# Pointwise convolution with a scaled weight: the weight set-up ahead of the main loop rewritten, and the first waits moved into the loop

## The chip, the cores and the metric

The kernel runs on one core of one Trainium2 chip. Its time is the device time of an execution in microseconds (us). A core has five engines that run side by side and wait for each other through semaphores: TensorE (PE in the profile; its weight loads are PEld), VectorE (DVE), ScalarE (ACT), GpSimd (POOL) and SyncE (SP), which here only issues DMA transfers.

## The reference

With a depthwise kernel of size 1, the padding is zero wide and the double loop runs once:

```python
H = W = 384; C = 384; k = 1           # x: (1, 384, 384, 384), dw: (1, 1, 384), pw: (384, 384), all bf16
out = out + xp[:, i:i+H, j:j+W, :] * dw[i, j][None, None, None, :]
return jnp.einsum('bhwc,cd->bhwd', out, pw)
```

So each of the 147456 pixels is a row of 384 channels, and the output row is `x * (diag(dw) @ pw)`: one matrix product of 147456 x 384 by 384 x 384. 113 MB are read and 113 MB written.

## The kernel before

**Tiles.** The pixels are cut into 288 supertiles of 512 rows. A supertile lies in SBUF with 4 rows on each of the 128 partitions. TensorE needs the channels on the partitions, so VectorE transposes it (L255) in 32 x 32 blocks of 32-bit words, each word holding two neighbouring channels. A transposed tile `T` thus has, on each group `q` of 32 partitions, channel pairs: block `b` (0 to 5) has 64 channels, and `par` (0, 1) picks the even or the odd ones. Each matmul multiplies 32 channels by the weight `w_r[32q : 32q+32, b, par, :]` and four of them, one for each `q`, run at once in the four row groups of the array, each into its own PSUM bank. Six blocks times two parities times four groups make 48 matmuls for a supertile, accumulated in PSUM.

**Main loop.** L222 to L225: 144 passes of two supertiles, the first with `T0` and PSUM set `PS[0]`, the second with `T1` and `PS[1]`. In `supertile` the matmuls of blocks 0 and 3 wait for the two halves of `T` (`s_t`), the first one for ScalarE to have emptied the PSUM set (`s_a`), and the last matmuls of blocks 2 and 5 signal `s_pe`. ScalarE copies each finished supertile from PSUM to the output tile `O` as bf16 (L296), VectorE transposes the supertile after next.

**Transfers.** SP issues, in order, `pw_n` (L131), seven loads of X of 1, 1, 2, 2, 4, 10 and 10 supertiles (L112), and then loads and stores as buffers come free. ScalarE issues the small `dw_row` (L130).

**Set-up of the weights**, the part that the change touches. `w_r` must hold `dw * pw`, with the rows permuted (even and odd channels apart) and repeated on all four partition groups:

- GpSimd fills `zero` and `ones` (L229, L230) and makes the 0/1 selection matrix `sel` with an affine select (L231).
- TensorE runs dummy matmuls on `zero` (`idle_work(2)`, L181: 16 of them), then three matmuls that turn `dw_row` into columns (L196, signal `s_df`), then 16 more dummy matmuls.
- VectorE copies the columns to `dw_f` (L273) and multiplies `sel` by them into `sel_w`, one 512-column product for each 128 rows of `pw` (L277, signal `s_sw`).
- TensorE multiplies `sel_w` and `pw_n` (L212): for each block `b` two full 128-row matmuls, of which each does the scaling, the permutation and the repetition for one parity. They wait for all of `pw_n` (`s_pw`), and blocks 4 and 5 reuse PSUM banks that must first be copied out.
- The copies from PSUM into `w_r` (`w_out`, L268), one of 768 columns for each block, are done by ScalarE for blocks 0, 2, 3, 4 and 5 and by VectorE for block 1 (`w_eng`), and signal `s_wr`.
- VectorE's first transposes stand behind its copy, in VectorE's own order.
- TensorE waits for the copies of blocks 0, 2 and 3 ahead of the loop (L221). The other waits for copies are attached to the first matmul of each block in the first supertile of a pass, so they are met in every pass and matter in the first only.

Of the kernel before, what the change touches and what calls it, by code (L numbers as in the profile page):

```python
# [7 lines left out]
BF16 = mybir.dt.bfloat16  # L8
F32 = mybir.dt.float32
# [17 lines left out]
def kernel(  # L27
# [12 lines left out]
    nc = tc.nc  # L40
    P = nc.NUM_PARTITIONS
    B, H, W, C = x.shape
    assert dw.shape[0] == 1 and dw.shape[1] == 1, "only k=1 depthwise supported"
    D = pw.shape[1]
    N = B * H * W
    assert C == 384 and D == 384 and N % 1024 == 0
    NB = C // 64
# [15 lines left out]
    consts = ctx.enter_context(tc.tile_pool(name="consts", bufs=1))  # L63
# [1 line left out]
    psum = ctx.enter_context(tc.tile_pool(name="psum", bufs=1, space=bass.MemoryType.PSUM))  # L65

    pw_n = consts.tile([P, 3, D], BF16, name="pw_n")
    ones = consts.tile([P, 4, P], BF16, name="ones")
    sel = consts.tile([P, 4, P], BF16, name="sel")
    sel_w = consts.tile([P, 3, 4, P], BF16, name="sel_w")  # L70
    w_r = consts.tile([P, NB, 2, D], BF16, name="w_r")
    dw_row = consts.tile([1, C], BF16, name="dw_row")
    dw_f = consts.tile([P, 3], F32, name="dw_f")
    warm = consts.tile([P, 3], F32, name="warm")
    zero = consts.tile([P, D], BF16, name="zero")

    Xs = [bufp.tile([P, 4 * LMAX, C], BF16, name=f"X{i}") for i in range(NR)]
    Ts = [bufp.tile([P, NB, 256], BF16, name=f"T{i}") for i in range(2)]
    Os = [bufp.tile([P, 4 * LMAX * D], BF16, name=f"O{i}") for i in range(NR)]
    PS = [psum.tile([P, 4, 512], F32, name=f"ps{s}") for s in range(2)]  # L80

    s_x = [[nc.alloc_semaphore(f"s_x{i}{k}") for k in range(max(map(len, groups[i::NR])))] for i in range(NR)]
    s_t = [[nc.alloc_semaphore(f"s_t{i}{h}") for h in range(2)] for i in range(2)]
    s_pe = nc.alloc_semaphore("s_pe")
    s_a = [nc.alloc_semaphore(f"s_a{i}") for i in range(2)]
    s_d = nc.alloc_semaphore("s_d")
    s_o = [nc.alloc_semaphore(f"s_o{i}") for i in range(NR)]
    s_dw = nc.alloc_semaphore("s_dw")
    s_pw = nc.alloc_semaphore("s_pw")
    s_df = nc.alloc_semaphore("s_df")  # L90
    s_sw = nc.alloc_semaphore("s_sw")
    s_dwf = nc.alloc_semaphore("s_dwf")
    s_sel = nc.alloc_semaphore("s_sel")
    s_w = nc.alloc_semaphore("s_w")
    s_wr = [nc.alloc_semaphore(f"s_wr{e}") for e in range(2)]
    s_seed = nc.alloc_semaphore("s_seed")
    s_zero = nc.alloc_semaphore("s_zero")

    with tc.tile_critical():  # L99
# [28 lines left out]


        nc.scalar.dma_start(dw_row[:], dw.rearrange("a e c -> a (e c)")).then_inc(s_dw, 16)  # L130
        nc.sync.dma_start(pw_n[:], pw.rearrange("(k p) d -> p k d", p=P)).then_inc(s_pw, 16)  # L131

        todo = []
        for t, (g, i, off, first, L) in enumerate(chunks):
# [9 lines left out]


        w_eng = [1, 0, 1, 1, 1, 1]
        w_done, made = [], [0, 0]
        for e in w_eng:
            made[e] += 1
            w_done.append((s_wr[e], made[e]))  # L150

        def w_ps(b):
            return PS[0 if b in (2, 3) else 1][:, 2 * (b % 2) : 2 * (b % 2) + 2, :D]


        def supertile(s, rv):
            for b in range(NB):
                for par in range(2):
                    for q in range(4):
                        if par == 0 and q == 0 and b in (0, 3):  # L160
                            nc.tensor.wait_ge(s_t[s][b // 3], rv)
                        mm = nc.tensor.matmul(  # L162
                            PS[s][:, q, :D],
                            lhsT=Ts[s][32 * q : 32 * q + 32, b, par::2],
                            rhs=w_r[32 * q : 32 * q + 32, b, par, :],
                            start=(b == 0 and par == 0),
                            stop=(b == NB - 1 and par == 1),
                            tile_position=(32 * q, 0),
                        )
                        if b == 0 and par == 0 and q == 0:  # L170
                            mm._wait_ge(s_a[s], rv)
                        elif s == 0 and q == 0 and par == 0:
                            mm._wait_ge(*w_done[b])
                        if b in (2, 5) and par == 1 and q == 3:
                            mm.then_inc(s_pe)


        def idle_work(n):
            with nc.tensor.Fori(0, n, 1) as _:
                for i in range(8):  # L180
                    nc.tensor.matmul(  # L181
                        PS[0][:, i % 4, :D],
                        lhsT=zero[32 * (i % 4) : 32 * (i % 4) + 32, 0:P],
                        rhs=zero[32 * (i % 4) : 32 * (i % 4) + 32, :],
                        start=True,
                        stop=True,
                        tile_position=(32 * (i % 4), 0),
                    )

        nc.tensor.wait_ge(s_zero, 1)  # L190
        idle_work(2)

        nc.tensor.wait_ge(s_dw, 16)
        nc.tensor.wait_ge(s_seed, 2)
        for k in range(3):
            mm = nc.tensor.matmul(  # L196
                PS[1][:, k, D : D + 1],
                lhsT=dw_row[:, P * k : P * k + P],
                rhs=ones[0:1, 0, 0:1],
                start=True,  # L200
                stop=True,
            )
        mm.then_inc(s_df)
        idle_work(2)
        nc.tensor.wait_ge(s_pw, 16)
        for b in range(NB):
            if b % 2 == 0:
                nc.tensor.wait_ge(s_sw, b // 2 + 1)
            if b >= 4:
                nc.tensor.wait_ge(*w_done[b - 4])  # L210
            for r in range(2):
                mm = nc.tensor.matmul(  # L212
                    w_ps(b)[:, r, :],
                    lhsT=sel_w[:, b // 2, 2 * (b % 2) + r, :],
                    rhs=pw_n[:, b // 2, :],
                    start=True,
                    stop=True,
                )
            mm.then_inc(s_w)
        for b in (0, 2, 3):  # L220
            nc.tensor.wait_ge(*w_done[b])  # L221
        with nc.tensor.Fori(0, NS // 2, 1) as it:  # L222
            rv = nc.tensor.to_reg(it + 1)
            for s in range(2):
                supertile(s, rv)  # L225
# [3 lines left out]
        nc.gpsimd.memset(zero[:].bitcast(U32), 0).then_inc(s_zero)  # L229
        nc.gpsimd.memset(ones[:], 1.0).then_inc(s_seed)  # L230
        nc.gpsimd.affine_select(  # L231
            out=sel[:].rearrange("p (v r) (q w) -> p v r q w", v=2, q=4),
            in_=ones[:].rearrange("p (v r) (q w) -> p v r q w", v=2, q=4),
            pattern=[[-64, 2], [-1, 2], [0, 4], [-2, 32]],
            compare_op=mybir.AluOpType.is_equal,
            fill=0.0,
            base=0,
# [8 lines left out]
        def transposes(t, j):  # L246
            g, i, off, first, L = chunks[t]
            jj = first + j
            s = jj % 2
            Xw = Xs[g % NR][:].bitcast(U32)[:, 4 * off : 4 * (off + L), :].rearrange("p (k l) c -> p k l c", l=L)  # L250
            Tw = Ts[s][:].bitcast(U32).rearrange("p b (i k) -> p b k i", k=4)
            for h in range(2):
                if h == 0 and j == 0:
                    nc.vector.wait_ge(s_x[g % NR][i], 16 * sum(len(ls) > i for ls in groups[g % NR : g + 1 : NR]))
                ins = nc.vector.transpose(  # L255
                    out=Tw[:, 3 * h : 3 * h + 3],
                    in_=Xw[:, :, j, 96 * h : 96 * h + 96].rearrange("p k (b w) -> p b k w", w=32),
                )
                if jj >= 2:
                    ins._wait_ge(s_pe, 2 * (jj - 2) + h + 1)  # L260
                ins.then_inc(s_t[s][h])

        order = [(t, j) for t in range(NT) for j in range(chunks[t][4])]

        def w_out(b):
            e = w_eng[b]
            out, in_ = w_r[:, b, :, :], w_ps(b)
            i = nc.vector.tensor_copy(out, in_) if e == 0 else nc.scalar.copy(out, in_)  # L268
            i._wait_ge(s_w, b + 1)
            i.then_inc(s_wr[e])  # L270

        nc.vector.wait_ge(s_df, 1)
        nc.vector.tensor_copy(dw_f[:].rearrange("p (k o) -> p k o", o=1), PS[1][:, 0:3, D : D + 1]).then_inc(s_dwf)  # L273
        nc.vector.wait_ge(s_sel, 1)
        nc.vector.wait_ge(s_dwf, 1)
        for k in range(3):
            nc.vector.tensor_scalar_mul(sel_w[:, k], sel[:], dw_f[:, k : k + 1]).then_inc(s_sw)  # L277
        for b in range(NB):
            w_out(b)
        transposes(*order[0])  # L280
        transposes(*order[1])

        for jj, (t, j) in enumerate(order):
            g, i, off, first, L = chunks[t]
            s = jj % 2
# [4 lines left out]
            if jj + 1 == NS:  # L290
                nq = 2
                nc.vector.wait_ge(s_o[g % NR], 16 * sum(map(len, groups[g % NR : g : NR])))
                e = nc.vector.tensor_copy(Ov[:, nq:4, j, :], PS[s][:, nq:4, :D])  # L293
# [37 lines left out]
```

## Time and profile before

| | us |
|---|---|
| median of 15 runs | 576.5 |
| lowest and highest | 575.62, 578.65 |
| profiled execution | 576.96 |
| span of its profile | 575.2 |

| engine | busy us | share of the span |
|---|---|---|
| PE | 568.2 | 99% |
| PEld | 418.7 | 73% |
| DVE | 507.5 | 88% |
| ACT | 418.9 | 73% |
| POOL | 1.7 | 0% |

The share of busy time is an average. For a change that touches the first 8 us alone, the timeline of these is what matters. The issue of DMA transfers there, by SP (start us, duration us):

```profile
1.01 0.45 SPq L131 DMA_DIRECT2D pw_n<-in_pw_dram  x1
1.53 3.90 SPq L112 DMA_DIRECT2D X<-in_x_dram  x7
```

A line of a group reads: line in the kernel, engine, operation, output and input tile, shape, number | busy time in us, mean duration of one in ns | idle time of the engine before them and what ended it. A line of the timeline reads: start, time from the first start to the last end, engine, line, operation, count, and in brackets the idle time before it. Matmuls overlap in the array, so durations of four concurrent ones are not added; the distance of their starts is the rate.

### The profile page before, as it was taken

The numbers are of one execution on the slowest core, as the hardware profiler recorded it, in microseconds if no ns is written. First come the engines' busy times: TensorE is split into PE (matmuls) and PEld (weight loads), VectorE is DVE, ScalarE is ACT, GpSimd is POOL, SyncE is SP. The second block draws the span as 40 slices with busy tenths as digits, with TensorE's granted clock in tenths as the row PEclk, the third lists the DMA queues.
The fourth block names the chain that finished last, engine by engine and source line by source line (L and its number), as shares of the span: only waits on it lengthen the run. The fifth ranks groups of instructions, "written<-read, shape, count | busy, mean of one in ns | idle before, by whom it ended". The sixth has DMA issues, their size and how long they took to land.

```text
span 575.2 us, 29707 instructions
## 1 busy us (share of the span) xinstructions
PE 568.2 (99%) x13871; PEld 418.7 (73%) x13871; DVE 507.5 (88%) x582; ACT 418.9 (73%) x296; POOL 1.7 (0%) x8
## 2 busy tenths in 40 slices
PE   8999999999999999999999999999999999999996
PEld 5777777777777777777777777777777777777774
DVE  6888898889988988898889888988898999888984
ACT  5777777777777777777777777777777777777775
POOL 1000000000000000000000000000000000000000
PEclk9999999999999999999999999999999999999999
DMA  8999999999999999999999999999999999994996
GB/s 320 432 414 420 427 412 428 432 424 401 382 425 402 383 400 426 391 406 391 430 390 396 396 432 391 391 402 421 398 381 414 410 389 395 420 392 149 389 408 264
DMA packets 25912, 226.88 MB, mean 394 GB/s; under 512 B 1197, under 2 KB 5678, under 8 KB 22062
## 3 DMA queue, kind: packets, MB, share of 16 engines
q1 hardware_dynamic: 25900, 226.79, 98.0%
q14 instruction: 9, 0.07, 0.0%
q8 instruction: 1, 0.02, 0.0%
q10 hardware_dynamic: 2, 0.00, 0.0%
HBM read 113.54 MB, written 113.25 MB: 394 GB/s over the span
## 4 chain that ended last, share of the span: by engine, by line
PE 98%; DMA 0%; ACT 0%; DVE 0%; issue 0%; POOL 0%; POOLq 0%; SPq 0%
PE ps L162 97%; PE ps L212 1%; PE ps L181 0%; DMA out_dram<-O 0%; ACT O L296 0%; DVE O L293 0%; POOL zero L229 0%; POOL warm L228 0%; POOLq L326 0%; PE ps L196 0%; SPq L99 0%
## 5 line engine op out<-in xcount | busy, mean ns | idle before, releaser
L162 PE MATMUL ps<-w_r,T 32*128 32x384 bf16 x13824 | 561.8, 321 | 0.4 <-issue 0.4
L255 DVE STREAM_TRANSPOSE T<-X 128x384 uint32<-128x384 uint32 x576 | 504.5, 877 | 56.0 <-DMA X<-in_x_dram 0.4
L162 PEld LDWEIGHTS ps<-w_r,T 32*128 32x128 bf16 x13824 | 415.9, 93 | 146.3 <-issue 0.8
L296 ACT CAST O<-ps 128x1536 bf16<-128x1536 f32 x288 | 413.6, 1436 | 148.1 <-PE ps L162 148.1
L268 ACT CAST w_r<-ps 128x768 bf16<-128x768 f32 x5 | 3.7, 811 | 2.4 <-PE ps L212 2.4
L181 PE MATMUL ps<-zero 32*128 32x384 bf16 x32 | 2.8, 516 | 1.4 <-POOL zero L229 1.4
L212 PE MATMUL ps<-pw_n,sel_w 128*128 128x384 bf16 x12 | 3.7, 498 | 0.0
L293 DVE CAST O<-ps 128x768 bf16<-128x768 f32 x1 | 1.0, 958 | 3.0 <-DMA out_dram<-O 3.0
L212 PEld LDWEIGHTS ps<-pw_n,sel_w 128*128 128x128 bf16 x12 | 1.6, 144 | 2.3 <-issue 1.7
L273 DVE COPY dw_f<-ps 128x3 f32<-128x3 f32 x1 | 0.2, 160 | 3.0 <-PE ps L196 3.0
L181 PEld LDWEIGHTS ps<-zero 32*128 32x128 bf16 x32 | 1.1, 118 | 2.0 <-issue 1.7
L241 ACT ACT_TABLE_LOAD x1 | 1.3, 1283 | 1.5 <-SPq L99 1.5
L268 DVE CAST w_r<-ps 128x768 bf16<-128x768 f32 x1 | 1.0, 958 | 1.5 <-PE ps L212 1.5
L277 DVE TENSOR_SCALAR sel_w<-sel,dw_f 128x512 bf16<-128x512 bf16 x3 | 0.9, 350 | 0.1
L231 POOL TENSOR_SCALAR_AFFINE_SELECT sel<-ones 128x512 bf16<-128x512 bf16 x1 | 0.7, 735 | 0.1
L196 PEld LDWEIGHTS ps<-ones,dw_row 1*128 1x128 bf16 x3 | 0.3, 127 | 0.3 <-issue 0.2
L230 POOL MEMSET ones<- 128x512 bf16 x1 | 0.5, 529 | 0.0
L241 ACT COPY warm<-warm 128x1 f32<-128x1 f32 x2 | 0.3, 188 | 0.0
L229 POOL MEMSET zero<- 128x192 uint32 x1 | 0.3, 258 | 0.0
L196 PE MATMUL ps<-ones,dw_row 1*128 1x1 bf16 x3 | 0.3, 174 | 0.0
L228 POOL MEMSET warm<- 128x3 f32 x1 | 0.1, 101 | 0.5 <-SPq L99 0.5
L315 POOL MEMSET const-bfloat16-1.0<- 128x1 bf16 x1 | 0.1, 101 | 0.0
(3 smaller groups left out, 0.3 us busy)
## 6 DMA issues: line engine op xcount, KB each, us to landing
X<-in_x_dram SPq DMA_DIRECT2D x26, 3840.0 KB, 20.9
out_dram<-O SPq DMA_DIRECT2D x26, 3840.0 KB, 26.4
X<-in_x_dram SPq DMA_DIRECT2D x2, 1536.0 KB, 17.6
out_dram<-O SPq DMA_DIRECT2D x2, 1536.0 KB, 14.1
X<-in_x_dram SPq DMA_DIRECT2D x3, 768.0 KB, 8.5
out_dram<-O SPq DMA_DIRECT2D x3, 768.0 KB, 8.9
X<-in_x_dram SPq DMA_DIRECT2D x1, 2304.0 KB, 19.1
out_dram<-O SPq DMA_DIRECT2D x1, 2304.0 KB, 13.0
```

The source lines that it names most:

```text
L162: mm = nc.tensor.matmul(PS[s][:, q, :D], lhsT=Ts[s][32 * q : 32 * q + 32, b, par::2], rhs=w_r[32 * q : 32 * q + 32, b, par, :], start=(b = ...
L181: nc.tensor.matmul(PS[0][:, i % 4, :D], lhsT=zero[32 * (i % 4) : 32 * (i % 4) + 32, 0:P], rhs=zero[32 * (i % 4) : 32 * (i % 4) + 32, :], s ...
L196: mm = nc.tensor.matmul(PS[1][:, k, D : D + 1], lhsT=dw_row[:, P * k : P * k + P], rhs=ones[0:1, 0, 0:1], start=True, stop=True,)
L212: mm = nc.tensor.matmul(w_ps(b)[:, r, :], lhsT=sel_w[:, b // 2, 2 * (b % 2) + r, :], rhs=pw_n[:, b // 2, :], start=True, stop=True,)
L230: nc.gpsimd.memset(ones[:], 1.0).then_inc(s_seed)
L231: nc.gpsimd.affine_select(out=sel[:].rearrange("p (v r) (q w) -> p v r q w", v=2, q=4), in_=ones[:].rearrange("p (v r) (q w) -> p v r q w" ...
L241: c = nc.scalar.copy(warm[:, s + 1 : s + 2], warm[:, 0:1])
L255: ins = nc.vector.transpose(out=Tw[:, 3 * h : 3 * h + 3], in_=Xw[:, :, j, 96 * h : 96 * h + 96].rearrange("p k (b w) -> p b k w", w=32),)
L268: i = nc.vector.tensor_copy(out, in_) if e == 0 else nc.scalar.copy(out, in_)
L277: nc.vector.tensor_scalar_mul(sel_w[:, k], sel[:], dw_f[:, k : k + 1]).then_inc(s_sw)
L293: e = nc.vector.tensor_copy(Ov[:, nq:4, j, :], PS[s][:, nq:4, :D])
L296: a = nc.scalar.copy(Ov[:, 0:nq, j, :], PS[s][:, 0:nq, :D])
```

## The change

- `pw_n` comes in three transfers of 128 rows, two issued by SP and the last by ScalarE, each with its own semaphore. Within each 128 rows the even rows go to partitions 0 to 63, the odd ones to 64 to 127.
- GpSimd makes a 128 x 128 identity `eye`; VectorE sums it over the four groups to `sel`, 128 x 32 in fp32. `sel_w` is its product with `dw_f`, repeated over the four groups by a broadcast operand: 128 columns for each 128 rows of `pw`, not 512.
- The dw columns come from twelve matmuls with 32 output partitions each, in the row order of the new `pw_n`.
- The dummy loop's body has 4 matmuls, not 8; it runs three times and once, not twice and twice.
- The weight copies are four concurrent 32-row matmuls for each 128 rows of `pw`. Each writes one of four (block, parity) pairs, so a copy out of PSUM now takes two blocks of one parity.
- The waits for the copies ahead of the loop are gone; in the first supertile of a pass, the first matmul waits for the first four copies, and blocks 4 and 5 are taken even parity first, with one wait for each parity.

```diff
-    sel = consts.tile([P, 4, P], BF16, name="sel")
-    sel_w = consts.tile([P, 3, 4, P], BF16, name="sel_w")
+    eye = consts.tile([P, P], BF16, name="eye")
+    sel = consts.tile([P, 32], F32, name="sel")
+    sel_w = consts.tile([P, 3, 4, 32], BF16, name="sel_w")
...
-        nc.sync.dma_start(pw_n[:], pw.rearrange("(k p) d -> p k d", p=P)).then_inc(s_pw, 16)
+        for k, eng in enumerate((nc.sync, nc.sync, nc.scalar)):
+            rows = pw[P * k : P * k + P, :].rearrange("(u r) d -> r u d", r=2)
+            eng.dma_start(pw_n[:, k, :], rows).then_inc(s_pw[k], 16)
...
+        w_first = {(0, 0): [(0, 1), (1, 3)], (4, 0): [(1, 4)], (4, 1): [(1, 5)]}
...
+        steps = [(b, par) for b in range(4) for par in range(2)] + [(4, 0), (5, 0), (4, 1), (5, 1)]
...
+            for b, par in steps:
+                for q in range(4):
+                    if q == 0 and par == 0 and b in (0, 3):
+                        nc.tensor.wait_ge(s_t[s][b // 3], rv)
+                    if q == 0 and s == 0:
+                        for e, v in w_first.get((b, par), []):
+                            nc.tensor.wait_ge(s_wr[e], v)
...
-                        elif s == 0 and q == 0 and par == 0:
-                            mm._wait_ge(*w_done[b])
...
-                for i in range(8):
+                for i in range(4):
...
-        idle_work(2)
-
+        idle_work(3)
+
...
+            for j in range(4):
+                r0 = P * k + 64 * (j % 2) + j // 2
                 mm = nc.tensor.matmul(
-                    w_ps(b)[:, r, :],
-                    lhsT=sel_w[:, b // 2, 2 * (b % 2) + r, :],
-                    rhs=pw_n[:, b // 2, :],
+                    PS[1][32 * j : 32 * j + 32, 0, D + k : D + k + 1],
+                    lhsT=dw_row[:, r0 : r0 + 63 : 2],
+                    rhs=ones[0:1, 0:1],
                     start=True,
                     stop=True,
+                    tile_position=(0, 32 * j),
+                )
+        mm.then_inc(s_df)
+        idle_work(1)
+        for k in range(3):
+            nc.tensor.wait_ge(s_pw[k], 16)
+            nc.tensor.wait_ge(s_sw, k + 1)
+            if k == 2:
+                nc.tensor.wait_ge(*w_done[0])
+                nc.tensor.wait_ge(*w_done[1])
+            for j in range(4):
+                mm = nc.tensor.matmul(
+                    PS[(k + 1) % 2][:, j, :D],
+                    lhsT=sel_w[32 * j : 32 * j + 32, k, :, :].rearrange("p q w -> p (q w)"),
+                    rhs=pw_n[32 * j : 32 * j + 32, k, :],
+                    start=True,
+                    stop=True,
+                    tile_position=(32 * j, 0),
                 )
             mm.then_inc(s_w)
-        for b in (0, 2, 3):
-            nc.tensor.wait_ge(*w_done[b])
...
+            out, in_ = w_r[:, 2 * k : 2 * k + 2, r, :], w_ps(i)
...
+            o._wait_ge(s_w, k + 1)
...
+        nc.vector.tensor_reduce(
+            out=sel[:],
+            in_=eye[:].rearrange("p (q w) -> p w q", q=4),
+            op=mybir.AluOpType.add,
+            axis=mybir.AxisListType.X,
+        ).then_inc(s_dwf)
         nc.vector.wait_ge(s_df, 1)
-        nc.vector.tensor_copy(dw_f[:].rearrange("p (k o) -> p k o", o=1), PS[1][:, 0:3, D : D + 1]).then_inc(s_dwf)
...
+        nc.vector.tensor_copy(dw_f[:], PS[1][:, 0, D : D + 3]).then_inc(s_dwf)
+        nc.vector.wait_ge(s_dwf, 2)
         for k in range(3):
-            nc.vector.tensor_scalar_mul(sel_w[:, k], sel[:], dw_f[:, k : k + 1]).then_inc(s_sw)
+            nc.vector.tensor_scalar_mul(
+                sel_w[:, k], sel[:].unsqueeze(1).to_broadcast([P, 4, 32]), dw_f[:, k : k + 1]
+            ).then_inc(s_sw)
```

In the new file the main loop's matmul is L168 (before L162), the dummy work L185 (L181), the dw matmuls L202 (L196), the weight copies' matmuls L219 (L212); the loop stands at L228 (L222). The program that results has, per pass of the loop, three stand-alone waits on TensorE as before: two at its head and one ahead of the second supertile (before: one at the head, one at block 3, one ahead of the second supertile). The waits attached to matmuls go from eight to six.

## The prediction

> **What bounds the kernel now.** I read the chain of waits of the whole execution first, then the groups of instructions, then the first 9 us piece by piece.
>
> ```profile
> PE 98%; DMA 0%; ACT 0%; DVE 0%; issue 0%; POOL 0%; POOLq 0%; SPq 0%
> PE ps L162 97%; PE ps L212 1%; PE ps L181 0%; DMA out_dram<-O 0%; ACT O L296 0%; DVE O L293 0%; POOL zero L229 0%; POOL warm L228 0%; POOLq L326 0%; PE ps L196 0%; SPq L99 0%
> ...
> L162 PE MATMUL ps<-w_r,T 32*128 32x384 bf16 x13824 | 561.8, 321 | 0.4 <-issue 0.4
> L255 DVE STREAM_TRANSPOSE T<-X 128x384 uint32<-128x384 uint32 x576 | 504.5, 877 | 56.0 <-DMA X<-in_x_dram 0.4
> ```
>
> The main loop (L162) is 97% of the chain and TensorE idles 0.4 us before it in all: once started it never waits. 561.8 us over 144 passes is 3.90 us a pass, or 162.5 ns for each four concurrent matmuls. So the end moves only if the loop starts at another time, runs at another rate, or the tail after it changes. The start-up, from the chain cut at 9 us (start, duration, what):
>
> ```profile
> 1.43 1.46 PE ps L181 x12
> 2.89 0.03 PE ps L196
> 2.92 1.30 PE ps L181 x10
> 4.22 3.67 PE ps L212 x12
> 7.88 0.39 issue
> 8.27 0.81 PE ps L162 x13
> ```
>
> Dummy work, the little dw matmuls, dummy work, the weight copies, 0.39 us of loop entry; the loop starts at 8.27. Beside it, the timelines of ScalarE and VectorE:
>
> ```profile
> 5.01 0.80 ACT L268 CAST w_r<-ps 128x768 bf16<-128x768 f32 x1 [1.94 <-PE ps L212]
> 6.29 2.91 ACT L268 CAST w_r<-ps 128x768 bf16<-128x768 f32 x4 [0.48 <-PE ps L212]
> ...
> 5.65 0.96 DVE L268 CAST w_r<-ps 128x768 bf16<-128x768 f32 x1 [1.52 <-PE ps L212]
> 6.59 6.71 DVE L255 STREAM_TRANSPOSE T<-X 128x384 uint32<-128x384 uint32 x8
> ```
>
> The loop entry stands behind ScalarE's third copy (ended 7.79). The first half of the first transposed tile was ready at 7.46. It started at 6.59 for two reasons at once: VectorE's copy ended at 6.61, and by the trace's landing events the last of the 16 parts of the first X load came at 6.56, 1.5 us after the other 15 (4.45 to 5.04).
>
> The array's clock is the second thing to see. The twelve L212 matmuls, by tile, and the clock after the loop, by stretches:
>
> ```profile
> L212 PE MATMUL ps<-pw_n,sel_w x12: 327/527/528, 4.2 to 7.6; 128*128 128x384 bf16 x12
> ...
> 574.00:574.07 0.07, 0.00 (x0) 0.00 (x0) 0.00 (x0) 0.00 (x0) 0.00 (x0) 1.00 0.00 0
> 574.08:574.20 0.12, 0.00 (x0) 0.00 (x0) 0.00 (x0) 0.00 (x0) 0.00 (x0) 0.50 0.00 0
> ```
>
> The L212 matmuls take 528 ns and start 0.32 us apart (384 columns at half rate) until 7.3; the last takes 327. The trace's clock record begins with full speed at 7.46 and falls to half between 574.07 and 574.08, 4 us after the last matmul.
>
> [...] matmuls ran from 1.43 on, which covers (4.05 - 1.43) / 3.41 = 77% of the window 0.64 to 4.05, yet the L212 matmuls after 4.05 were at half rate. 77% was not enough; the next window, full, was. [...]
>
> **The change part by part.** Times are on the span's axis of this profiled execution (span 575.2, time 576.96; it lies 0.46 above the median 576.5, and I carry a difference over to the median).
>
> *pw in three transfers.* SP issues two instead of one (0.45 us each), so each of its X issues is 0.45 later; ScalarE issues the third, which puts its table load (1.28 us) and warm copies from 2.78 to about 3.3, well before its first copy. The same 288 KB lie ahead of X. The first third can land earlier than 4.10, the landing that released L212; at best near 3.3, where the first part landed. X's landing: from no shift (bytes bound it) to +0.45 (issue bounds it). I take no shift.
>
> *Dummy and dw work.* 16 dummy matmuls become 12 and 16 become 4. Fours start 0.32 apart, but in a loop of four the branch shows: the second pass of before loaded weights 0.4 us after the first. I get 1.43, 1.84, 2.25, done near 2.57, as the fourth four of before began at 2.34. Then 12 dw matmuls of 32 columns, not 3. Spacing of before: 26 to 70 ns, so 0.3 to 0.8 us; I take 0.45. Last start 3.05, plus 0.19 (start to signal, as before): 3.25 against 2.95. VectorE from there to the first sel_w took 0.66 (2.95 to 3.61). The new sel_w has a quarter of the elements, but from fp32; bounds 0.5 to 0.7, I keep 0.66: 3.9. The reduction and eye stand before that, hidden under the dw wait (VectorE idles 2.97 us there; the select alone cost 0.7 and gets smaller).
>
> *Weight copies.* Twelve full matmuls become three fours: 12 x 0.32 = 3.84 becomes 3 x 0.32 = 0.96 at half clock. First four at 4.0; from a last start to its signal took 0.54 (4.44 to 4.98), so 4.57 instead of 4.98. ScalarE's copies then run back to back, 0.69 apart (6.29, 6.98, 7.67): the third ends at 4.59 + 1.38 + 0.81 = 6.78. TensorE's entry into the loop is past by then (the third four waits only for VectorE's copy, 4.59 + 0.96 = 5.55), so the 0.39 issue goes and a wake of 0.15 remains: 6.95 by weights.
>
> *What is late next.* X. VectorE is free at 5.55; with the landing of 6.56 the first transposed half is ready at 6.57 + 0.87 = 7.44, and the loop starts at 7.56. With a landing of 5.1 it is 6.95; with 7.0, 8.0. I take 7.56: 0.71 earlier than 8.27.
>
> *Waits in the loop.* Pass for pass the stand-alone waits of L161's kind stay three (51 ns each in the trace): one more at the head, one fewer at block 3, and two fewer waits attached to matmuls. The sequencer reaches the head 0.59 us before the array does. Cost 0; if that cover were gone, 144 x 0.07 = 10 us, but the count argues against it. The order of blocks 4 and 5 keeps the number of matmuls and the signals at half and end; later copies (third 6.78, last 8.2) are done before blocks 4 and 5 are reached.
>
> *The clock.* This pays it back. The array now has dummy work to about 3.6, then only three fours (0.96 us) until the loop. In the grid of this trace the window 4.05 to 7.46 is busy for some 30%, less than the 77% that failed, so it is not released at 7.46; 7.46 to 10.88 is busy 97%. So the loop runs at half rate from 7.56 to 10.88 and falls back by 3.32 / 2 = 1.66 us. Bounds: 0 if released before the start, (14.29 - 8.0) / 2 = 3.1 if a late start spoils one more window. The net is -0.71 + 1.66 = +0.95. Transposes and copies keep pace with a slower array; the tail stays.
>
> Sum: 576.96 + 0.95 = 577.9 in this execution's grid, so 576.5 + 0.95 = 577.4 for the median. Some 0.2%, 1.15 us, is what a measurement of this kernel can tell from no change; this lies inside.
>
> **Rivals.**
> 1. *Clock released in time.* Little activity might suffice in some grids, or the 77% might have failed for another reason. Then the start counts in full: -0.71 (X at 6.56) to -1.32 (X early), 575.2 to 575.8. For: ScalarE's chain surely gets shorter. Against: the 77%. A gain beyond about 1.6 meets the second X tiles: the third supertile's load landed at 9.56 and would be wanted at about 8.6.
> 2. *X late into a missed window: slower.* If the extra SP issue shows in full (landing 7.0), the loop starts at 8.0, the window to 10.88 is 84% busy. Where more than 84% is needed, release comes at 14.29: -0.27 + 3.1 = +2.9, 579.4. In a grid that merely puts the first full window half a window later than 10.88, it is (12.6 - 8.0) / 2 - 0.27 = +2.0, 578.5. It decides from a start of 8.0, or from a release after about 11.3. For: packets of that X load that took over 1 us; a free grid. Against: the other 15 parts landed by 5.04.
> 3. *Nothing moves:* X as before and a release near 9: under 0.3 either way, 576.5.
>
> **How the numbers follow.** The forecast's mechanism (a gain at the start, given back by the clock) 0.55, with own range 576.3 to 578.4; it lies mostly within 0.2%, and about two in five of it beyond. Rival 1: 0.22, somewhat more than half of it faster by over 0.2%. Rival 2: 0.15, all slower. Rival 3: 0.08, same. Faster 0.14, same 0.47, slower 0.39. The range takes in rival 1's ends and the milder form of rival 2: 575.3 to 578.6.
>
> **What would show it.** Right: in the profile after, L219 as three fours ending near 4.6 for the first; ScalarE's third copy done near 6.8; the loop's first matmul between 6.95 and 8.0, waiting for T; its first matmuls at 520 ns and 0.32 apart; a clock release some 3 us after the loop's start; then 3.90 us a pass. Wrong: first loop matmuls at 321 ns (then rival 1), a pass other than 3.90 us, the loop starting at 8.3 or later, or idle time in front of L168.

## The result, and the profile after

The changed kernel takes 584.4 us (median of 6 runs, 583.8 to 585.72) against 576.5: a ratio of 1.0139, 95% interval 1.0128 to 1.0151. It is slower by 8 us, well outside the predicted range of 575.3 to 578.6. The profiled execution took 584.99 with a span of 583.3.

The page of the changed kernel, chain of waits by engine and by line, and the groups that answer to those shown of before:

```profile
PE 96%; DMA 2%; ACT 1%; DVE 0%; SPq 0%; issue 0%
PE ps L168 96%; DMA pw_n<-in_pw_dram 2%; DMA out_dram<-O 0%; ACT w_r L274 0%; ACT O L310 0%; DVE O L307 0%; SPq L134 0%; PE ps L219 0%; SPq L340 0%; SPq L100 0%
...
L168 PE MATMUL ps<-w_r,T 32*128 32x384 bf16 x13824 | 564.4, 322 | 1.4 <-ACT w_r L274 1.4
L261 DVE STREAM_TRANSPOSE T<-X 128x384 uint32<-128x384 uint32 x576 | 505.3, 878 | 62.3 <-DMA X<-in_x_dram 4.8
L219 PE MATMUL ps<-pw_n,sel_w 32*128 32x384 bf16 x12 | 1.3, 505 | 8.1 <-DMA pw_n<-in_pw_dram 8.1
```

A transfer, that of `pw_n`, has come into the chain with 2% of the span, and the twelve weight matmuls, now only 1.3 us of work, waited 8.1 us for it. VectorE waited 4.8 us for X, where it had waited 0.4. The chain cut at 16 us (start, duration, what) puts it in order of time:

```profile
1.01 0.70 SPq L134
1.71 0.06 issue
1.77 10.15 DMA pw_n<-in_pw_dram
11.92 0.05 issue
11.96 0.53 PE ps L219 x4
12.50 0.02 issue
12.52 1.51 ACT w_r L274 x2
14.03 0.14 issue
14.16 2.08 PE ps L168 x19
```

One 96 KB transfer ends 10.15 us after its issue, and the loop starts at 14.16 instead of 8.27: 5.89 us of the loss. The rest is in the loop's first pass. By stretches of 3.90 us from the start of the loop, the length of one pass in the steady state, first of the kernel before, then of the changed one (columns: stretch, length, busy time and number of instructions of PE, PEld, DVE, ACT and POOL, recorded clock, DMA share, GB/s):

```profile
8.27:12.17 3.90, 3.90 (x96) 2.89 (x100) 3.69 (x5) 2.36 (x3) 0.00 (x0) 1.00 1.04 438
```

```profile
14.16:18.06 3.90, 3.90 (x52) 2.21 (x56) 2.45 (x4) 1.27 (x2) 0.00 (x0) 1.00 1.08 458
```

52 matmuls instead of 96 in the same time: the array runs at half rate. (The clock column shows 1.00 where the trace has no clock record yet; the count of matmuls is what tells.) The trace's clock record begins at 19.47. From the first matmul of the first pass to that of the second it is 6.49 us, every later pass is 3.90. The tail, from the start of the last matmul to the end of the span, is 5.51 us before and 5.07 after: the last part of the last store landed 0.45 us sooner. So 5.89 + 2.59 = 8.48 us, less 0.44 in the tail, is the difference of the spans, 8.0.

Why is the transfer slow? The two views of the DMA engines over the first 12 us, in 40 slices of 0.3 us, before and then after (tenths of the 16 engines' time; GB/s):

```profile
DMA  0000000649999998999335599899999999999999
GB/s 0 0 0 0 0 0 3 115 100 292 343 399 410 399 359 328 328 369 215 102 123 215 236 389 420 369 410 389 410 410 451 410 471 492 430 430 471 410 451 451
```

```profile
DMA  0000000030000111959999997865967999999999
GB/s 0 0 0 0 0 0 3 0 15 0 0 0 20 46 46 49 220 141 374 405 405 361 351 371 200 266 251 184 430 220 261 320 358 276 340 297 364 371 389 430
```

From 2.7 to 5.4 us the kernel before moves 292 to 410 GB/s. After, there are 0.9 us (3.9 to 4.8) at 46 to 49 GB/s, with one tenth of the engines busy: two of sixteen. The landing events agree. Each transfer reports the landing of its parts: a third of `pw` has one report within 0.7 us of the end of its issue and then only two late ones (6.36 and 6.44; 10.34 and 10.49; 11.88 and 11.92), and of the first X load 14 parts land by 6.90, the other two at 12.74 and 12.79. Two engines carry all of `pw`, each with a packet of 768 bytes every 33 ns, and the share of X that they also carry lands behind it. The size of the packets is not the cause: the kernel before loads `pw` in packets of 768 bytes too, and its 16 parts have landed by 4.10.

At 46.5 GB/s the 288 KB of `pw` would take an estimated 6.3 us (294912 bytes over that rate). The last part lands later, at 11.92. From 2.7 to 3.6 us no data moves, and from 4.8 on packets of X run too; how the remaining time divides was not measured.

### The profile page after: what moved, and what is told of

Read it like the earlier page. It is cut to its first block, busy times and chain, and to the rows that moved or that the text cites. A ratio compares the mean times of both kernels' runs of the same rounds, so it can differ in the third digit from the quotient of the medians.

```text
span 583.3 us, 29696 instructions
## 1 busy us (share of the span) xinstructions
PE 567.7 (97%) x13864; PEld 380.6 (65%) x13864; DVE 508.4 (87%) x583; ACT 418.8 (72%) x296; POOL 0.9 (0%) x8
## 4 chain that ended last, share of the span: by engine, by line
PE 96%; DMA 2%; ACT 1%; DVE 0%; SPq 0%; issue 0%
PE ps L168 96%; DMA pw_n<-in_pw_dram 2%; DMA out_dram<-O 0%; ACT w_r L274 0%; ACT O L310 0%; DVE O L307 0%; SPq L134 0%; PE ps L219 0%; SPq L340 0%; SPq L100 0%
## 5 line engine op out<-in xcount | busy, mean ns | idle before, releaser
L168 PE MATMUL ps<-w_r,T 32*128 32x384 bf16 x13824 | 564.4, 322 | 1.4 <-ACT w_r L274 1.4
L168 PEld LDWEIGHTS ps<-w_r,T 32*128 32x128 bf16 x13824 | 379.6, 93 | 186.3 <-issue 1.9
L219 PE MATMUL ps<-pw_n,sel_w 32*128 32x384 bf16 x12 | 1.3, 505 | 8.1 <-DMA pw_n<-in_pw_dram 8.1
L219 PEld LDWEIGHTS ps<-pw_n,sel_w 32*128 32x128 bf16 x12 | 0.4, 99 | 8.9 <-DMA pw_n<-in_pw_dram 8.9
L185 PE MATMUL ps<-zero 32*128 32x384 bf16 x16 | 1.9, 494 | 1.4 <-POOL zero L235 1.4
L185 PEld LDWEIGHTS ps<-zero 32*128 32x128 bf16 x16 | 0.5, 100 | 2.0 <-issue 2.0
L202 PEld LDWEIGHTS ps<-ones,dw_row 1*32 1x32 bf16 x12 | 0.2, 101 | 0.3 <-issue 0.3
L202 PE MATMUL ps<-ones,dw_row 1*32 1x1 bf16 x12 | 0.2, 167 | 0.0
```

Source lines behind the costliest of these rows:

```text
L168: mm = nc.tensor.matmul(PS[s][:, q, :D], lhsT=Ts[s][32 * q : 32 * q + 32, b, par::2], rhs=w_r[32 * q : 32 * q + 32, b, par, :], start=(b, ...
L185: nc.tensor.matmul(PS[0][:, i, :D], lhsT=zero[32 * i : 32 * i + 32, 0:P], rhs=zero[32 * i : 32 * i + 32, :], start=True, stop=True, tile_p ...
L202: mm = nc.tensor.matmul(PS[1][32 * j : 32 * j + 32, 0, D + k : D + k + 1], lhsT=dw_row[:, r0 : r0 + 63 : 2], rhs=ones[0:1, 0:1], start=Tru ...
L219: mm = nc.tensor.matmul(PS[(k + 1) % 2][:, j, :D], lhsT=sel_w[32 * j : 32 * j + 32, k, :, :].rearrange("p q w -> p (q w)"), rhs=pw_n[32 * ...
```

## The experiments

Lines of diff are against the changed kernel unless said otherwise.

### The row order of the transfer

The change reads each third of `pw` as `(u r) d -> r u d` with r = 2. So the slowest dimension of the source is 2, and in the trace each third has two late parts. Three runs test whether the row order is what leaves the transfer to two engines.

`natural_rows`: no even/odd order.

```diff
-            rows = pw[P * k : P * k + P, :].rearrange("(u r) d -> r u d", r=2)
-            eng.dma_start(pw_n[:, k, :], rows).then_inc(s_pw[k], 16)
+            eng.dma_start(pw_n[:, k, :], pw[P * k : P * k + P, :]).then_inc(s_pw[k], 16)
```

> The changed kernel with one thing undone: each third of pw is read in its natural row order, 128 rows to 128 partitions, still three transfers on the same two queues. The rows then pair with other channels than the selection expects, so the weights are permuted; the amount of work is the same. Theory A (the even/odd row order makes the transfer's outermost dimension 2, and so only two DMA engines carry it: in the trace of the changed kernel two of 16 parts of every later X load land 6 us late): pw parts land by about 4, the first X load with all 16 parts by about 7, the loop starts between 7 and 8, and the time falls from 584.4 to 576.5 to 578. Theory B (three transfers on two queues, or the X loads issued later, are the cause whatever the row order): the pw thirds still land near 6, 10 and 12 us and the time stays within 583.5 to 585.5.

Measured: 577.58 us (22 runs), ratio to before 1.0017 (1.0007 to 1.0027). Sixteen parts of each third now land, by 3.00, 4.28 and 4.08, and X's sixteen parts by 6.24. The row order of the transfers alone was worth 6.8 us. Theory A holds.

`before_strided`, against the kernel before: only the transfers of the change.

```diff
-        nc.sync.dma_start(pw_n[:], pw.rearrange("(k p) d -> p k d", p=P)).then_inc(s_pw, 16)
+        for k, eng in enumerate((nc.sync, nc.sync, nc.scalar)):
+            rows = pw[P * k : P * k + P, :].rearrange("(u r) d -> r u d", r=2)
+            eng.dma_start(pw_n[:, k, :], rows).then_inc(s_pw[k], 16)
...
+            if b % 2 == 0:
+                nc.tensor.wait_ge(s_pw[b // 2], 16)
```

> The kernel before with one thing of the change added: pw comes in the three transfers in even/odd row order (two by SP, one by ScalarE), and each pair of blocks waits for its third. The dw factors and the selection keep the old row order, so the weights are permuted; the amount of work is the same. Theory A (two engines): the thirds land near 6.4, 10.5 and 11.9 us, the first X load near 12.8, eight full weight matmuls of 0.32 us follow 11.9, the loop starts near 14 to 15.5, time 582.5 to 585.5. Theory B (the new weight matmuls, the shorter dummy work or the waits in the loop are the cause): 576 to 577.5.

Measured: 584.72 us, ratio 1.0137 (1.0115 to 1.0159): this one part alone costs as much as the whole change. The sum is not quite the same: the loop starts still later, at 14.94, its first pass loses 0.43 us in place of 2.59, and the tail is 6.24 us. Its chain of waits, cut at 16 us:

```profile
1.78 10.32 DMA pw_n<-in_pw_dram
12.09 0.05 issue
12.14 2.74 PE ps L215 x8
14.88 0.06 issue
14.94 1.08 PE ps L164 x9
```

The same 10 us of transfer stand in front of the old weight matmuls.

`halves`: even and odd rows as transfers of 64 rows each, so that the slowest dimension is 64.

```diff
...
+            for r, eng in enumerate((nc.sync, nc.scalar)):
+                eng.dma_start(pw_n[64 * r : 64 * r + 64, k, :], rows[r]).then_inc(s_pw[k], 16)
```

> The changed kernel with each third of pw fetched as two transfers of 64 rows, even rows and odd rows, one issued by SP and one by ScalarE, so that the outermost dimension of each is 64 and the row order is kept: the whole computation. Theory A (two engines): all pw by about 4.5, X issued from about 2.5 us on, loop start 7 to 8, time 576 to 578. Theory B (number of transfers and queues): six transfers are worse than three, 585 or more. On the clock: if the array is released only after a window that is busy for more than 77%, the first passes run at half rate for 2 to 4 us after the loop's start and this kernel is not faster than the kernel before; if it is released earlier, 575 to 576.

Measured: 579.27 us, ratio 1.0042 (1.0025 to 1.0059): 5 us better than the change and far from the 585 of theory B, but above the 576 to 578 of theory A. Six issues put X's first issue at 3.01, its landing at 7.47, the loop at 8.46; and the first pass took 5.62 us. The profiled execution was the slowest of the seven (580.83), with a tail of 7.48 us, 1.97 longer than in the profile of the kernel before. None of these three (start, first pass, tail) comes from the two engines.

### The clock

natural_rows starts its loop at 7.22, 1.05 us before the kernel before does, and is still not faster. Its first pass is 6.57 us and the clock record begins at 12.68. By stretches, natural_rows:

```profile
7.22:11.12 3.90, 3.90 (x52) 2.18 (x56) 2.82 (x4) 0.60 (x1) 0.00 (x0) 1.00 1.04 436
```

The forecast and the expectations speak of windows of the clock. Two traces give their length. The record of full speed runs from 7.46 to 574.08 before and from 19.47 to 582.67 in the change; the two lengths, 566.61 and 563.20 us, differ by 3.41 us, and a step of 3.413 us goes 166.0 and 165.0 times into them. So I count windows in steps of 3.413 us back from the release, the start of that record. Their place in the span differs between executions: the first whole one starts at 0.64 before and at 2.83 in rows64. In the kernel before, TensorE worked for 2.62 of the 3.41 us from 0.64 to 4.05, 77%, and the matmuls after that still took 528 ns; it worked through all of the next window, and the release came at its end, 7.46.

If the clock takes the gain, keeping the array at work until the loop must bring it back. `pairs` computes everything, with four transfers (64 rows of the first third each, then 64 x 2 rows); `pairs_warm` adds work for the array, dummy matmuls and repeats of the weight matmuls; `pairs_waits_ahead` moves the first waits back ahead of the loop.

```diff
...
+        for k0, k1 in ((0, 1), (1, 3)):
+            rows = pw[P * k0 : P * k1, :].rearrange("(k u r) d -> r u k d", r=2, u=64)
+            for r, eng in enumerate((nc.sync, nc.scalar)):
+                eng.dma_start(pw_n[64 * r : 64 * r + 64, k0:k1, :], rows[r]).then_inc(s_pw[k0], 16)
```

> The changed kernel with pw in four transfers whose outermost dimension is 64: even and odd rows of the first 128 rows, then even and odd rows of the other 256, on SP and ScalarE; the whole computation. Theory (what the last runs left: the start is earlier, the array is not): X's loads land as with the natural row order, the loop starts at 7.0 to 7.6, 0.7 to 1.3 earlier than before, the first pass takes 5.5 to 6.7 us instead of 3.90, the time is 576.9 to 578.2. Rival (the new weight matmuls win once the transfer is mended): 575.0 to 576.0.

> The kernel of 'pairs' with the array kept at work from 1.4 us to the loop: small dummy matmuls before the first weight four, between the first and the second and just ahead of the loop, the second weight four done twice and the third four times into the same banks before their signals. Clock theory (the array is released after a window that is nearly all busy; 77% was too little[...]): release by 7.6, the first pass 3.90 to 4.4 us, loop start 6.9 to 7.5, time 575.0 to 576.0, some 1.5 to 2 below 'pairs'. Rival (the slow first passes have another cause, such as the loads of X or the waits at the head of the loop): first pass still 5.5 us or more, and the added work delays the start: 577.5 to 579.

> The kernel of 'pairs' with the waits for the first four weight copies back ahead of the loop, where TensorE meets them before it enters the loop. Theory: the loop's start is set by the first X load and its transpose, the copies end 0.5 us or more before, so the loop entry of 0.4 us stays hidden: the same as 'pairs' within 0.3 us. Rival (the waits inside the loop cost in every pass): 144 times 10 ns or more is saved, the passes fall below 3.90 us, and it is 1.4 us or more faster than 'pairs'.

Measured: pairs 578.4 us, ratio 1.0033 (1.0022 to 1.0044); pairs_warm 578.04, 1.0025 (1.0012 to 1.0038); pairs_waits_ahead 578.7, 1.0036 (1.0024 to 1.0047). The starts missed what I expected. In pairs 31 of the 32 parts of the second pair of transfers landed by 4.63 and the last at 6.50, and the loop started at 8.75. In pairs_warm that landing was 5.54, and the work added ahead of the loop took the start to 8.59. The first pass took 5.30 us in pairs, just below the 5.5 to 6.7 expected, and 4.13 in pairs_warm, as expected, though the release came at 9.08 and not by 7.6. As times, the two are the same within their intervals. In the two profiles pairs_warm is 1.34 us ahead at the end of the first pass and loses 0.68 of it in a longer tail; why the medians are only 0.36 apart is not known.

The waits, by the chains of pairs and pairs_waits_ahead ahead of the loop:

```profile
7.11 1.51 ACT w_r L275 x2
8.62 0.14 issue
8.75 3.35 PE ps L169 x36
```

```profile
7.01 1.51 ACT w_r L277 x2
8.52 0.43 issue
8.95 3.06 PE ps L169 x30
```

0.14 us from the last copy to the first matmul with the waits inside the loop, 0.43 with the waits ahead of it. All later passes are 3.90 us in both. The rival, a cost in each pass, is out; the edit saves 0.29 us where the copies are what the loop waits for, as these two profiles have it; the medians, 0.3 apart, are the same within their intervals.

`two` and `two_warm`: all of `pw` in two transfers, without and with work for the array; `two_sp_warm`: both on SP.

```diff
...
+        rows = pw.rearrange("(k u r) d -> r u k d", r=2, u=64)
+        for r, eng in enumerate((nc.sync, nc.scalar)):
+            eng.dma_start(pw_n[64 * r : 64 * r + 64, :, :], rows[r]).then_inc(s_pw[0], 16)
```

> The changed kernel with all of pw in two transfers whose outermost dimension is 64, even rows by SP and odd rows by ScalarE, so that X is issued near 1.5 to 1.7 as before; every weight four waits for both. All of pw by 3.8 to 4.3 (later if one part straggles, as one of 32 did in 'pairs' by 1.9 us), loop start 7.0 to 7.8, first pass 5.2 to 6.7 us, time 576.7 to 578.3. If the X issues were what held 'pairs' back, it is 0.5 to 1 faster than that; if stragglers among the parts hold it, the same.

> The kernel of 'two' with the array kept at work as in the kernel before: 16 dummy matmuls before the dw matmuls, 20 after them up to about 4.2 us, the second weight four done twice and the third three times into the same banks before their signals. Clock theory: the window that ends before 7.6 or 8.3 is more than 85% busy, so first pass 3.90 to 4.3 us, time 1 to 1.5 below 'two' and at or below the kernel before: 575.2 to 576.5. Rival (the start is what matters, and the added work delays it as much as the clock gains): the same as 'two'.

> The kernel of 'two_warm' with both transfers of pw on SP, ahead of X in the same queue. In 'two' the half on ScalarE's queue landed at 4.5 to 5.3, and in 'two_warm' as late as 6.8, beside X's packets, the half on SP by 3.9. If the queue beside X is what delays it: all of pw by 4.4, loop start 6.9 to 7.6, first pass 3.90 to 4.3 us, 575.3 to 576.4. If parts straggle on any queue: pw at 5 or later, loop start past 8, 577.5 or more.

Measured: two 578.83 us, ratio 1.0049 (1.003 to 1.0069); two_warm 578.54, 1.0035 (1.0021 to 1.0049); two_sp_warm 578.02, 1.0023 (1.0014 to 1.0033). All three lie above the range first given for them. In two the half on SP landed by 3.87, that on ScalarE's queue by 5.33, beside X's packets; in two_warm by 6.83; on SP both, by 4.90. That is better but still 0.8 us behind the 4.10 of the single transfer of before.

In two_warm the time is what the rival gave, the same as two, but not for the rival's reason. Its first pass is 1.57 us shorter and its loop starts 1.49 later; from the last part of `pw` to the loop it is 2.95 us, in two 2.96, so the late part delayed it and not the added work. In two_sp_warm the loop starts at 7.85, 0.14 us behind ScalarE's third copy, and the first pass still takes 5.28 us: the array waited for `pw` and for a copy, so that the window of the clock that ends at 7.28 was only 70% busy. So what stood in the expectation of two_sp_warm as the rival, late parts on any queue, explains part of it. Why single parts come 0.5 to 2 us late was not settled.

The cleanest test is on the transfers of natural_rows, which land early. In `natural_warm`, `fill(n)` runs n times four dummy matmuls of 128 columns, and the second and third weight four are repeated:

```diff
...
+        fill(3)
         for k in range(3):
...
+            for j in ((0, 1, 2, 3), (0, 1, 2, 3) * 2, (0, 1) + (0, 1, 2, 3) * 3)[k]:
...
+            if k == 0:
+                fill(3)
+        nc.tensor.wait_ge(*w_done[2])
+        nc.tensor.wait_ge(*w_done[3])
+        fill(4)
         with nc.tensor.Fori(0, NS // 2, 1) as it:
```

> The kernel of 'natural_rows' (weights permuted in the same way) with the array kept at work: small dummy matmuls before the first weight four, between first and second and just ahead of the loop, the second weight four done twice and the third three times before their signals. It sets the clock apart from the transfers, which land early here. Clock theory: release by 8.0, loop start 6.9 to 7.4, first pass 3.90 to 4.3, time 575.0 to 576.2, that is 1.4 to 2.4 below natural_rows (577.58) and below the kernel before (576.5). Rival (the slow first pass comes from X's loads): first pass stays above 5.5 us, 577.5 or more.

Measured: 575.58 us (12 runs, 575.47 to 576.99), ratio to before 0.9982 (0.997 to 0.9993), and 2.0 us below natural_rows, whose runs spread from 576.19 to 580.71. By stretches, natural_warm: the first pass, then the two windows of the clock's grid that end before its release at 7.65.

```profile
7.30:11.20 3.90, 3.90 (x100) 2.71 (x97) 2.52 (x4) 2.31 (x3) 0.00 (x0) 1.00 1.05 437
0.83:4.24 3.41, 2.81 (x56) 1.46 (x56) 1.24 (x6) 1.60 (x4) 0.73 (x4) 1.00 0.55 145
4.24:7.65 3.41, 3.18 (x57) 1.45 (x50) 2.98 (x4) 3.25 (x5) 0.00 (x0) 1.00 1.01 367
```

The loop starts 0.08 us later than in natural_rows, its first pass takes 4.05 us instead of 6.57, and the tail is 5.06 us in both. The start did not change, the rate did. The clock theory holds.

### A version that keeps both gains

`rows64` computes everything. It takes natural rows, which landed in sixteen parts for each third by 4.28 in natural_rows, and picks the parities with 64-row matmuls, two at once, in place of 32-row ones; selection, dw columns and `sel_w` are those of the kernel before.

```diff
+            for r in range(2):
+                if k == 2:
+                    nc.tensor.wait_ge(*w_done[r])
+                for _ in range(2 if (k, r) == (2, 1) else 1):
+                    for v in range(2):
+                        mm = nc.tensor.matmul(
+                            PS[(k + 1) % 2][:, 2 * r + v, :D],
+                            lhsT=sel_w[64 * v : 64 * v + 64, k, 2 * v + r, :],
+                            rhs=pw_n[64 * v : 64 * v + 64, k, :],
...
+                            tile_position=(64 * v, 0),
```

> A version that keeps what helped and computes everything: pw in three transfers of 128 rows in natural order (16 engines each), the weight copies as two concurrent 64-row matmuls for each parity in place of four 32-row ones, so that both parities can be picked from natural rows, the selection and dw columns of the kernel before, the waits inside the loop, and the array kept at work to the loop. It is the kernel of 'natural_warm' with twice the weight matmul time. Theory (start and clock explain all): pw thirds by 3.0, 4.3 and 4.4, first copy signalled near 4.2, loop start 6.9 to 7.5, first pass 3.90 to 4.3 us, 575.2 to 576.2, 0.5 or more below the kernel before. Rival (the gain of natural_warm came from its permuted weights or needs the 32-row fours): 576.5 or more.

Measured: 575.37 us (18 runs), ratio 0.9985 (0.9976 to 0.9993): 1.1 us below the kernel before, 9.0 below the change. Its chain ahead of the loop:

```profile
3.79 0.47 PE ps L228 x2
4.26 0.02 issue
4.28 2.26 ACT w_r L286 x3
6.54 0.14 issue
6.68 0.40 PE ps L195 x16
7.08 0.06 issue
7.14 4.87 PE ps L166 x113
```

The first copy starts at 4.28 instead of 5.01, three copies on ScalarE end at 6.53 instead of 7.79, and the loop starts at 7.14 instead of 8.27. Every pass is 3.90 us, the first too, as the clock was released at 6.24. The earlier start, 8.27 - 7.14 = 1.13, is the gain of the median, 1.1. The profiled execution itself shows little of it: it took 576.78, as its tail is 6.44 us. With the 5.06 that most profiles have it would have been at an estimated 575.4, the median, and that of the kernel before at 576.5.

### All runs in one table

All columns but the last are from the profiled execution, one for each kernel; the fifth is half the distance from start to release, the sixth the first pass less 3.90, the seventh the time from the start of the last matmul to the end of the span.

| kernel | loop start | release | first pass | (release - start) / 2 | measured excess | tail | profiled us | median us |
|---|---|---|---|---|---|---|---|---|
| before | 8.27 | 7.46 | 3.90 | 0 | 0 | 5.51 | 576.96 | 576.5 |
| the change | 14.16 | 19.47 | 6.49 | 2.65 | 2.59 | 5.07 | 584.99 | 584.4 |
| before_strided | 14.94 | 15.86 | 4.33 | 0.46 | 0.43 | 6.24 | 584.78 | 584.72 |
| natural_rows | 7.22 | 12.68 | 6.57 | 2.73 | 2.67 | 5.06 | 578.12 | 577.58 |
| natural_warm | 7.30 | 7.65 | 4.05 | 0.18 | 0.15 | 5.06 | 575.68 | 575.58 |
| halves | 8.46 | 11.98 | 5.62 | 1.76 | 1.72 | 7.48 | 580.83 | 579.27 |
| pairs | 8.75 | 11.64 | 5.30 | 1.44 | 1.40 | 5.07 | 578.4 | 578.4 |
| pairs_warm | 8.59 | 9.08 | 4.13 | 0.25 | 0.23 | 5.75 | 577.74 | 578.04 |
| pairs_waits_ahead | 8.95 | 12.85 | 5.80 | 1.95 | 1.90 | 5.07 | 579.12 | 578.7 |
| two | 8.29 | 12.68 | 6.04 | 2.19 | 2.14 | 5.06 | 578.66 | 578.83 |
| two_warm | 9.78 | 10.98 | 4.47 | 0.60 | 0.57 | 5.06 | 578.62 | 578.54 |
| two_sp_warm | 7.85 | 10.69 | 5.28 | 1.42 | 1.38 | 5.49 | 577.89 | 578.02 |
| rows64 | 7.14 | 6.24 | 3.90 | 0 | 0 | 6.44 | 576.78 | 575.37 |

Two events, the loop's first matmul and the release, give each first pass to within 0.06 us. Loop start, excess and tail, with some 561.46 us for the matmuls between, give each span. The code of the tail is the same in all kernels; it ends with the last part of the last store, which landed 3.73 to 6.15 us after the start of the last matmul.

## Why the prediction was wrong, and where it was right

**The step that failed** is "pw in three transfers": "The same 288 KB lie ahead of X", "X's landing: from no shift (bytes bound it) to +0.45 (issue bounds it)". The thirds landed at 6.44, 10.49 and 11.92, and X at 12.79, where I had the first third by 4.10 at most and X by 7.0. I counted the bytes, over all engines together, and did not ask how many of these one transfer uses. The diff showed `(u r) d -> r u d` with r = 2; that this left two engines, at 46 to 49 GB/s, is what the runs show, and neither end of my bounds contained it. The rival that I gave for a slower kernel, X late by half a microsecond, had the direction and the missed clock window, but not the wait: the first half of T was ready at 13.67, while the loop stood behind ScalarE's third weight copy (ended 14.02) and so behind `pw`. The term of the transfers made all of the loss beyond the forecast: without it, natural_rows measured 577.58 against my 577.4.

**The clock** was right as a mechanism: with the array kept at work, natural_warm had its release at 7.65 and a first pass of 4.05 us, natural_rows at 12.68 and 6.57. In the change it took 2.59 us where I had 1.66, as the start lay elsewhere in the grid. For the kernel without the slow transfer I had a start 0.71 earlier and 1.66 given back; the profile of natural_rows shows 1.05 and 2.67. Both terms were too small, by 0.34 and 1.01 us, and pull opposite ways; with a tail 0.45 us shorter, which I had as unchanged, the sum is +1.2 in that execution, and +1.1 in the median, against my +0.95. That it came out so near is in part luck. The half-rate windows fit the 77% that failed in the kernel before: in the change the window 12.64 to 16.06 was 60% busy (2.05 of 3.42 us) and no release came at its end, in pairs 8.22 to 11.64 was 85% busy (2.89 of 3.42 us) and one came.

```profile
12.64:16.06 3.42, 2.05 (x29) 1.08 (x29) 2.93 (x4) 2.79 (x4) 0.00 (x0) 1.00 1.07 450
```

```profile
8.22:11.64 3.42, 2.89 (x40) 1.61 (x44) 2.16 (x4) 1.79 (x3) 0.00 (x0) 1.00 1.06 446
```

**Dummy and dw work.** I had the dw signal at 3.25, 0.3 later than before, for twelve matmuls at up to 70 ns; it came at 2.99 against 2.95. Twelve in groups of four cost almost nothing. `sel_w` was ready at 3.51 instead of my 3.9.

**Weight copies.** In natural_rows, where the transfers don't cover it, the first four started at 3.65 (I had 4.0), the third copy ended at 6.41 (6.78). The gain was right in kind and 0.37 larger.

**What is late next.** X and its transpose, as said: in natural_rows the loop waited for T, with X's last part at 6.24 and the other fifteen by 5.30. My start of 7.56 was 7.22 there.

**Waits in the loop.** Cost 0 in each pass, as said, though the lead of the sequencer over the array at the head of a pass, on which I relied, fell from 0.59 to 0.25 us; entry 0.43 to 0.14 us, against 0.39 and 0.15.

**Rival 1**, a release in time, does not happen with the short dummy work: in all five kernels that have that work and start by 9 us (natural_rows, halves, pairs, pairs_waits_ahead, two) the release came 2.9 to 5.5 us after the start. With the array kept at work it comes 0.36 us after the start in natural_warm and 0.90 before it in rows64, and natural_warm is then where rival 1 put it, 575.58.

## What to carry to other kernels

When a diff rearranges a transfer, look at the outermost dimension of its source before counting bytes: a split by 2 there left two DMA engines at work here, at 46 to 49 GB/s, and what these engines carried later waited as well (two of the sixteen parts of the first X load landed at 12.74 and 12.79, the others by 6.90). In this kernel a start 1.05 us earlier was lost because TensorE was not at full clock when the loop began (2.67 us); so count the share of each clock window in which it works (82% brought no release here, 85% did), and fill the holes, with repeated or dummy matmuls in banks that nobody reads. Test such parts one at a time on data movement that is sound: in the change the slow transfer started the loop 5.89 us later and hid the gain of 1.05 us that natural_rows shows.

## What the runs showed that I had not expected

Two engines moved 46 to 49 GB/s, 23 to 24 each, with packets of 768 bytes 33 ns apart. In these thirteen profiles a release of the clock took a window that was nearly all busy, by the busy time of TensorE: the busiest that brought none had 82% (0.83 to 4.24 in natural_warm, 0.74 to 4.15 in two_warm), the least busy that brought one 85% (pairs). The spread of a kernel's times may hang on it too (575.47 to 575.68 for ten of the twelve runs of natural_warm, 576.19 to 580.71 for natural_rows), but this is not shown: the tail alone lay between 5.06 and 7.48 us in these profiles. And single parts of a transfer landed 0.5 to 2 us behind the others in most profiles (X in before at 6.56 against 5.04, the second pair in pairs at 6.50 against 4.63), and so did the last store in halves; a start-up that waits for the last part of several transfers meets this often. Its cause was not tried.
